# Fourth pair's q and k converted in the transfer, and new copy and slot orders, in an attention kernel that feeds a two-layer product

## The chip, the cores and the metric

The kernel runs on one core of a Trainium2 chip. The metric is device time of one execution in microseconds (us), the median of the runs, lower is better. Times inside an execution come from a profile of one execution, counted from the start of its span.

## What is computed

There are 8 batches of 8 heads, 576 positions and 64 elements to a head. For each head:

```
cum    = cumsum(max(s, 0))
scores = q @ k.T / 8 + min(-(cum[i] - cum[j]), 0)     # only j <= i
x      = softmax(scores) @ v                          # heads side by side: 4608 x 512
h      = x @ w_in                                     # 512 -> 2048
out    = (h * clip(h + 3, 0, 6) / 6) @ w_out          # 2048 -> 512
```

Inputs and output are float32.

## The kernel before, in words

**Pairs and slots.** The work goes by pairs of heads, 32 of them, four to a batch (`PPB` = 4). The loop over `p` (L718) has one slot for each pair. In slot `p` the kernel computes the scores of pair `p` for head 0 and then head 1, its exponentials, the product with the values (`av`, one head behind), the division (`norm`), the transposed x (`transpose_x`), and it prepares q and k of pair `p+1` (`get(0)` for q, `get(1)` for k). Slots count from 0: the fifth slot is `p == 4`, the eighth is `p == 7`.

**The two-layer product.** From slot 4 on, `group()` puts one piece of it between the pieces of attention, by a list written out by hand (`plan`, L505) and, when it is used up, by what is ready. A piece is either `m1` (four matmuls into a bank `ph`, then a Relu on ScalarE into `tr` and a product on VectorE into `gT`) or `m2` (four matmuls into a bank `po`).

**Ways of q and k.** `flat(p)` (L104) says which of two layouts a pair has. A flat pair is loaded as float32 in pieces of 64 elements by SyncE into `raw` (L119) and cast to float16 `tok` by `cast_qk` (L182), on GpSimd unless another engine is given. Pairs below `PPB` are flat and so are those from `NPE` = 11 on. The others are loaded by GpSimd's queue with the conversion in the transfer, straight into `tok`, six positions to a partition on 96 partitions (L114). TensorE transposes a flat pair with five transposes of 128 (L226) for each of q and k, another with six of 96 (L233); pairs from 11 on are transposed by a DMA (`crossbar_qk`, L263). Then q and k are copied from PSUM, or from the DMA's `jt`, into `qk`. A flat pair needs two copies each, by `order` (L203 to L215), for the even and odd blocks. The others need two each at L250, for the even and odd positions, and the first of k is always ScalarE's (L247). `spread` (L267) is the name of the copies from `jt`.

**Bias rows.** Sums of s are computed for 32 heads at a time by `cum1` to `cum6`: a clip, a scan on VectorE (`cum2`), and a split into float16 parts in `rows_of`. The first set is made at the start (L674 to L693), the second in slots 10 to 13 (L763 to L776). `load_aug` (L139) brings a pair's rows into `qk`, by 2 transfers.

**Banks.** The transposes of q and k and of x go to PSUM banks by `t_bank` (L198): while `m2` has not begun, one of two banks `po` if the caller asks for the other one, else the bank `t`, which has one buffer.

**Queues.** The schedule is manual: each engine works its instructions off in the order of the program, and a DMA issue stands in the queue of the engine that issues it. At the start, GpSimd has the casts of the second pair, the values of the first, the third pair's casts, the second pair's values, the issues of the fifth pair (L709 to L714), then in slot 1 the bias rows of the fifth pair and the fourth pair's casts (L729, L730), and in slot 2 the first part of `w_in`. SyncE has bias rows, third pair, values and fourth pair (L700 to L708).

**The start.** ScalarE clips a part of s (L684) and casts the first pair (L688). VectorE makes the sums, and `pick` (L665) the rows in a form for pair 0. The first pair's q and k are each copied half by VectorE and half by ScalarE (L695, L696).

Of the kernel before, what the change touches and what calls it, by code (L numbers as in the profile page):

```python
# [18 lines left out]
def kernel(  # L19
# [10 lines left out]
    nc = tc.nc  # L30

    B, H, SEQ, D = q.shape
# [6 lines left out]
    PPB = H // 2  # L39
# [4 lines left out]
    NPE = 2 * PPB + 3  # L44
    NQK = 4
    NVA = 3
    NPROD = 2 * PPB
# [54 lines left out]
    toks = {}  # L102

    def flat(p):  # L104
        return p < PPB or p >= NPE

    def load_qk(p, i, eng=nc.sync):
        b, h0 = p // PPB, 2 * (p % PPB)
# [68 lines left out]
    def cast_qk(p, copy=nc.gpsimd.tensor_copy):  # L177
        tok = work.tile([128, 24 * D], F16, tag="tok", bufs=4, name="tok")
        toks[p] = tok[:, 0 : 18 * D]
        for i in range(2):  # L180
            c = slice(9 * D * i, 9 * D * (i + 1))
            copy(out=toks[p][:, c], in_=raws[p % NRAW][:, c])  # L182

    def cast_v(p):
        vraw, va = vraws[p % NRAW], vas[p % NVA]
        nc.gpsimd.tensor_copy(out=va[:, :, 0:4, 0:64], in_=vraw[:, :, 0:4, :])  # L186
        nc.gpsimd.tensor_copy(out=va[0:64, :, 4, 0:64], in_=vraw[0:64, :, 4, :])
# [10 lines left out]
    def t_bank(other, name):  # L198
        if not done[2] and other:
            return psum.tile([128, 640], F16, tag="po", bufs=2, name=name)  # L200
        return psum.tile([128, 640], F16, tag="t", name=name)
# [15 lines left out]
    def transpose(p, i, copies=(nc.vector.tensor_copy, nc.vector.tensor_copy)):  # L217
        transpose_out(p, i, transpose_in(p, i), copies)

    def transpose_in(p, i):  # L220
        tok = toks[p]
        pt = t_bank(i == 1, "pt")
        if flat(p):
            for c in range(5):
                c0 = 512 * i + 128 * c
                nc.tensor.transpose(  # L226
                    pt[:, 128 * c : 128 * (c + 1)], tok[:, c0 : c0 + 128], ident
                )
            return pt
        for hh in range(2):  # L230
            for c in range(3):
                n = 96 * (3 * hh + c)
                nc.tensor.transpose(  # L233
                    pt[:, n : n + 96],
                    tok[:, i, hh, 2 * c : 2 * c + 2, :].rearrange("p e d -> p (e d)"),
                    ident[0:96, 0:96],
                )
        return pt

    def transpose_out(  # L240
        p, i, pt, copies=(nc.vector.tensor_copy, nc.vector.tensor_copy)
    ):
        qk = qks[p % NQK]
        if flat(p):
            order(qk, i, pt.rearrange("p (t c) -> p t c", c=128), i, copies)
            return
        copies = (nc.scalar.copy if i else copies[0], copies[1])  # L247
        for par in range(2):
            to = qk[0:64, 0, i, par : par + SEQ]
            copies[par](  # L250
                out=bass.AP(
                    to.tensor,
                    to.offset,
                    [list(to.ap[0]), [2 * SPAD + 64, 2], [6, 96], [2, 3]],
                ),
                in_=pt[64 * par : 64 * par + 64, 0:SEQ].rearrange(
                    "p (h c t) -> p h t c", h=2, c=3
                ),
            )
# [381 lines left out]
    def cum2(n):  # L641
        C["c"] = work.tile([128, SEQ], F32, tag="c8", bufs=1, name="c8")
        nc.vector.tensor_tensor_scan(
            out=C["c"], data0=one.to_broadcast([128, SEQ]), data1=C["p"], initial=0.0, op0=ALU.mult, op1=ALU.add
        )
# [39 lines left out]
        out=C["p"][:, 304:SEQ], in_=C[0][:, 304:SEQ], func=AF.Relu, scale=8.0  # L685
    )
    cum2(0)
    cast_qk(0, nc.scalar.copy)  # L688
    cum3(0, V)
    nc.gpsimd.tensor_copy(out=rows_of[0][0:32, 0, 0:SEQ], in_=C["c"][0:32])  # L690
    cum4(0, V)
    cum5(0, V)
    cum6(0, V)  # L693
    pick(0)
    transpose(0, 0, (V.tensor_copy, nc.scalar.copy))  # L695
    transpose(0, 1, (V.tensor_copy, nc.scalar.copy))  # L696
    warm(NWARM[1])
    for g in range(1, 2 * NROW):
        pick(g)
# [2 lines left out]
        load_qk(2, i)  # L702
    load_aug(2, nc.sync)
    load_v(1, nc.sync)
    for i in range(2):
        load_qk(3, i)
    load_v(2, nc.sync)
    load_aug(3, nc.sync)  # L708
    cast_qk(1)  # L709
    cast_v(0)  # L710
    cast_qk(2)
    cast_v(1)
    for i in range(2):
# [4 lines left out]
    for p in range(NP):  # L718
        nxt = p + 1 < NP
        if NPE <= p + 3 < NP:  # L720
            for i in range(2):
                load_qk(p + 3, i)
        def qk_ahead():
            if PPB < p + 3 < NPE:
                for i in range(2):
                    load_qk(p + 3, i)

        if p == 1:
            load_aug(4, nc.gpsimd)  # L729
            cast_qk(3)  # L730
        elif p == 2:
            load_w_in(0)
            cast_v(2)
            qk_ahead()
        elif p == 3:
            cast_v(3)
            load_w_in(1)
            cast_v(4)
            qk_ahead()
            load_aug(5, nc.gpsimd)  # L740
        elif p:
            qk_ahead()
            if NPE <= p + 2 < NP:
                cast_qk(p + 2)
                crossbar_qk(p + 2)
            for fn, c in {
                4: ((I, 2),),
                5: ((I, 3),),
                6: ((U, 0), (U, 1), (U, 2), (U, 3)),
                7: ((U, 4), (U, 5), (U, 6), (U, 7)),  # L750
            }.get(p, ()):
                fn(c)
            if nxt:
                cast_v(p + 1)
            if NPROD <= p + 2 < NPROD + NQK:
                set_stair((p + 2) % NQK, nc.gpsimd.tensor_copy)
            if p + 2 < NP:
                load_aug(p + 2, nc.gpsimd)
        if p + 3 < NP:
            load_v(p + 3, nc.sync)  # L760
        if p == 2:
            nc.sync.dma_start(out=stair_sb, in_=stair_dram.ap())
        if p == 10:  # L763
            load_s(1, (nc.sync,) * 4)
            fill(nc.gpsimd, rows_of[1][:, 0, :], 1.0)
        if p == 11:
            cum1(1, nc.gpsimd)
        if p == 12:
            cum2(1)
            nc.gpsimd.tensor_copy(out=rows_of[1][0:32, 0, 0:SEQ], in_=C["c"][0:32])  # L770
        if p == 13:
            cum3(1, nc.gpsimd)
            cum4(1, nc.gpsimd)
        if p == 13:
            cum5(1, nc.gpsimd)
            cum6(1, nc.gpsimd)  # L776

        def get(i):
            if p + 1 < NPE:
                transpose(p + 1, i)  # L780
            elif nxt:
                spread(p + 1, i)

        if p < PPB:
            scores(p, 0, 0)
            scores(p, 0, 1)
            get(0)
            scores(p, 0, 2)
            corner(p)
            if p:  # L790
                av(p - 1, 1, 0)
                av(p - 1, 1, 1)
                norm(p - 1, 1)
            get(1)
            scores(p, 1, 0)
            scores(p, 1, 1)
            av(p, 0, 0)
            scores(p, 1, 2)
            if p:
                transpose_x(p - 1)  # L800
            av(p, 0, 1)
            norm(p, 0)
            continue

        if p == PPB:
            early[0] = False
            scores(p, 0, 0)
            av(p - 1, 1, 0)
            av(p - 1, 1, 1)
            norm(p - 1, 1)  # L810
            m1_begin(0, 0, NKC - 1)
            scores(p, 0, 1)
            transpose_x(p - 1)
            m1_begin(0, 1, NKC - 1)
            pt = transpose_in(p + 1, 0)
            scores(p, 0, 2)
            group()
            group()
            transpose_out(p + 1, 0, pt)
        else:  # L820
            if p == NPROD:
                nc.vector.tensor_scalar(
                    out=masks, in0=shut, scalar1=65504.0, scalar2=None, op0=ALU.add
                )
            scores(p, 0, 0)
            get(0)
            group()
            scores(p, 0, 1)
            av(p - 1, 1, 0)
            group()  # L830
            scores(p, 0, 2)
            av(p - 1, 1, 1)
            norm(p - 1, 1)
            group()
        corner(p)
        group()
        if p > NPE:
            x_done[0] = p - 1
        scores(p, 1, 0)
        if p < NPROD - 1:  # L840
            get(1)
            group()
        else:
            if p <= NPROD:
                transpose_x(p - 1)
            group()
            get(1)
        scores(p, 1, 1)
        av(p, 0, 0)
        if PPB < p < NPROD - 1:  # L850
            transpose_x(p - 1)
        elif p > NPROD:
            crossbar_x(p - 1)
        group()
        scores(p, 1, 2)
        group()
        av(p, 0, 1)
        norm(p, 0)
        group()
# [40 lines left out]
```

## Time and profile before

| what | before |
|---|---|
| time, median of 3 runs | 362.35 us (361.83 to 363.53) |
| span of the profiled execution | 361.3 us |
| mean granted TensorE clock | 0.994 |
| DMA moved | 51.60 MB, mean 143 GB/s |
| issue to landing, `raw` q by SyncE | 3.9 us (median) |
| issue to landing, `tok` q by GpSimd | 5.7 us (median) |
| issue to landing, `w_in` part by GpSimd | 9.3 us (median) |

In the profile, engines are PE (TensorE matmul), PEld (its weight load), DVE (VectorE), ACT (ScalarE), POOL (GpSimd) and SP (SyncE); a q behind the name is its sequencer. A line such as `L451 PE MATMUL ph<-xT,w_in_sb` names the code line, the engine, the operation, what it writes and what it reads. Square brackets tell how long the engine was idle ahead of it and what released it. Where a view merges several instructions, x2 is their number.

### The profile page before, as it was taken

The numbers are of one execution on the slowest core, as the hardware profiler recorded it, in microseconds if no ns is written. First come the engines' busy times: TensorE is split into PE (matmuls) and PEld (weight loads), VectorE is DVE, ScalarE is ACT, GpSimd is POOL, SyncE is SP. The second block draws the span as 40 slices with busy tenths as digits, with TensorE's granted clock in tenths as the row PEclk, the third lists the DMA queues.
The fourth block names the chain that finished last, engine by engine and source line by source line (L and its number), as shares of the span: only waits on it lengthen the run. The fifth ranks groups of instructions, "written<-read, shape, count | busy, mean of one in ns | idle before, by whom it ended". The sixth has DMA issues, their size and how long they took to land.

```text
span 361.3 us, 7738 instructions
## 1 busy us (share of the span) xinstructions
PE 348.6 (96%) x2919; PEld 192.9 (53%) x2919; DVE 250.5 (69%) x545; ACT 218.2 (60%) x382; POOL 131.3 (36%) x224
## 2 busy tenths in 40 slices
PE   8879999999999999999999999999999999999995
PEld 3666665555555555555555555555555444444442
DVE  8656997797898878677768777778674644544531
ACT  3757997577666666666666666666665343344310
POOL 5495679973656343515242515252000000000000
PEclk9989999999999999999999999999999999999999
DMA  9899999959999999999897969695122101101111
GB/s 182 170 175 216 217 208 204 182 129 174 179 220 173 226 176 216 193 169 183 181 184 172 199 150 197 158 206 141 21 76 20 58 2 58 59 2 58 58 59 60
DMA packets 152078, 51.60 MB, mean 143 GB/s; under 512 B 139864, under 2 KB 147080, under 8 KB 152040
## 3 DMA queue, kind: packets, MB, share of 16 engines
q1 hardware_dynamic: 141640, 43.74, 60.7%
q0 software_dynamic: 8992, 6.79, 11.7%
q10 hardware_dynamic: 1408, 0.57, 0.7%
q8 instruction: 23, 0.38, 0.5%
q14 instruction: 15, 0.12, 0.1%
HBM read 37.36 MB, written 9.44 MB: 130 GB/s over the span
## 4 chain that ended last, share of the span: by engine, by line
PE 84%; DVE 6%; DMA 4%; SPq 2%; POOL 1%; issue 1%; ACT 1%; POOLq 0%; DVEq 0%; ACTq 0%
PE po L478 33%; PE ph L451 32%; PE O L385 7%; PE S L315 6%; PE S L304 3%; DMA raw<-in_q_dram 2%; DMA jt<-tok 1%; DVE qk L250 1%; DVE gT L467 1%; DVE x L408 1%; DVE qk L210 1%; PE pt L233 1%; DMA vraw<-in_v_dram 1%; PE ptx L422 1%; SPq L119 1%
## 5 line engine op out<-in xcount | busy, mean ns | idle before, releaser
L467 DVE SCALAR_TENSOR_TENSOR gT<-tr,ph 128x512 f16<-128x512 f32 x144 | 98.8, 687 | 77.7 <-ACT tr L466 76.6
L451 PE MATMUL ph<-xT,w_in_sb 128*128 128x512 f16 x576 | 147.9, 379 | 0.5 <-DVE gT L467 0.4
L478 PE MATMUL po<-w_out_sb,gT 128*128 128x512 f16 x576 | 145.8, 379 | 0.0
L466 ACT ACTIVATE tr<-ph,bias 128x512 f32<-128x512 f32 x144 | 98.8, 687 | 73.6 <-PE ph L451 71.4
L334 ACT ACTIVATE P<-S 128x512 f16<-128x512 f32 x192 | 111.7, 595 | 45.9 <-PE S L304 25.0
L451 PEld LDWEIGHTS <-w_in_sb 128*128 128x128 f16 x576 | 51.7, 97 | 44.8 <-issue 0.7
L478 PEld LDWEIGHTS <-gT 128*128 128x128 f16 x576 | 50.0, 98 | 45.8 <-issue 0.2
L182 POOL CAST tok<-raw 128x576 f16<-128x576 f32 x48 | 32.3, 678 | 98.9 <-DMA raw<-in_q_dram 88.6
L315 PE MATMUL S<-qk 68*128 68x448 f16 (+3 forms) x256 | 49.4, 274 | 0.0
L385 PE MATMUL O<-va,P 128*128 128x65 f16 x896 | 48.4, 194 | 0.0
L385 PEld LDWEIGHTS <-P 128*128 128x128 f16 x896 | 39.9, 98 | 13.7 <-DVE qk L210 0.2
L315 PEld LDWEIGHTS <-qk 68*128 68x128 f16 x256 | 23.7, 99 | 22.9
L408 DVE TENSOR_TENSOR x<-O,rl 128x320 f16<-128x320 f32 x64 | 31.5, 491 | 2.2
L210 DVE COPY qk<-jt 64x768 f16<-64x768 f16 x84 | 31.6, 376 | 1.6
L142 POOL DMA_DIRECT2D qk<-rows_of x56 | 32.5, 582 | 0.0
L494 DVE TENSOR_SCALAR ob<-po 128x512 f32<-128x512 f32 (+1 forms) x36 | 24.3, 675 | 8.2 <-PE po L478 7.7
L304 PEld LDWEIGHTS <-qk 128*128 128x128 f16 (+1 forms) x256 | 19.4, 98 | 16.5 <-DVE qk L210 2.8
L304 PE MATMUL S<-qk 128*128 128x128 f16 (+1 forms) x256 | 25.6, 221 | 2.1 <-DVE qk L210 1.6
L186 POOL CAST va<-vraw 128x512 f16<-128x512 f32 x32 | 20.5, 641 | 11.2 <-PE O L385 7.3
L336 DVE TENSOR_TENSOR P<-P,shut 128x512 f16<-128x512 f16 x48 | 22.4, 467 | 2.0 <-ACT P L334 1.5
L250 DVE COPY qk<-pt 64x576 f16<-64x576 f16 x21 | 16.7, 801 | 2.0 <-ACT qk L250 1.6
L407 DVE RECIPROCAL rl<-O 128x5 f32<-128x5 f32 x64 | 12.1, 190 | 6.0 <-PE O L385 5.9
(71 smaller groups left out, 177.8 us busy)
## 6 DMA issues: line engine op xcount, KB each, us to landing
out_dram<-ob SPq DMA_DIRECT2D x35, 256.0 KB, 2.0
vraw<-in_v_dram SPq DMA_DIRECT2D x64, 128.0 KB, 4.9
raw<-in_q_dram SPq DMA_DIRECT2D x25, 288.0 KB, 3.9
raw<-in_k_dram SPq DMA_DIRECT2D x24, 288.0 KB, 4.4
w_in_sb<-in_moe_w_in_dram POOLq DMA_DIRECT2D x4, 512.0 KB, 9.3
w_out_sb<-in_moe_w_out_dram POOLq DMA_DIRECT2D x8, 256.0 KB, 8.5
vraw<-in_v_dram SPq DMA_DIRECT2D x32, 32.0 KB, 3.5
tok<-in_q_dram POOLq DMA_DIRECT2D x7, 144.0 KB, 5.7
```

Of the source, the lines that this page charges most:

```text
L142: eng.dma_start(out=qks[p % NQK][64:68, hh, :, 64 * hh : 64 * hh + SEQ], in_=rows_of[g // 32].rearrange("(r g) i t -> g r i t", g=32)[g % ...
L182: copy(out=toks[p][:, c], in_=raws[p % NRAW][:, c])
L210: copies[par](out=qk[0:64, :, i, 128 * par : 128 * par + 256 * n].rearrange("p h (s two c) -> p h s two c", two=2, c=128)[:, :, :, 0, :], ...
L304: mm(S[:, c], lhsT=kT[rows, c], rhs=qT[rows, c], start=(j == 0 and not by_product), stop=(j == 3),)
L315: mm(S[:, c : c + w], lhsT=kT[0:68, 128 * j : 128 * (j + 1)], rhs=qT[0:68, 128 * (j + 1) : SEQ], start=(c == 0), stop=(c != 0 and p >= NROW),)
L334: nc.scalar.activation(out=pt[:, c], in_=S, func=AF.Exp, scale=0.125)
L385: mm(o[:, i, :], lhsT=lhsT, rhs=va[:, hh, j, 0:65], **kw)
L408: nc.vector.tensor_tensor(out=X[p][:, :, hh, :], in0=o[:, :, 0:64], in1=rl.to_broadcast([128, 5, 64]), op=ALU.mult,)
L451: mm(ph, lhsT=w_in_sb[:, kc, ft * 128 : (ft + 1) * 128], rhs=xT[:, kc, n * 512 : (n + 1) * 512], start=(kc == 0), stop=(kc == NKC - 1),)
L466: nc.scalar.activation(out=tr, in_=ph, func=AF.Relu, bias=bias3[:, 0:1])
L467: nc.vector.scalar_tensor_tensor(out=gTs[n][:, ft, :], in0=tr, scalar=6.0, in1=ph, op0=ALU.min, op1=ALU.mult)
L478: mm(po, lhsT=gTs[n][:, ft, t4 * 128 : (t4 + 1) * 128], rhs=w_out_sb[:, ft, :], start=(ft == 0), stop=(ft == NFT - 1),)
```

## The change

The fourth pair (`p == 3`) leaves the flat layout: it is loaded with the conversion in the transfer, after the first pair's values are cast, and has no casts on GpSimd. In the first pair all of q is copied by ScalarE and all of k by VectorE; a cast of bias rows moves from GpSimd to ScalarE. In slot 4, a copy of the next q goes ahead of the first piece of the two-layer product and the first values' product goes ahead of the second head's scores. Slot 7 gets the order of slots 5 and 6, with the next k transposed ahead of a piece and x transposed after the values' product; the bank of the next k is changed for it. From slot 10 on, the copies of the next k go ahead of a piece. The second set of bias sums is begun a slot sooner. The purpose is to have fewer waits in the first slots and in those where the sums are made.

```diff
@@ -102,7 +102,7 @@
     toks = {}
 
     def flat(p):
-        return p < PPB or p >= NPE
+        return p < PPB - 1 or p >= NPE
 
     def load_qk(p, i, eng=nc.sync):
         b, h0 = p // PPB, 2 * (p % PPB)
@@ -219,7 +219,7 @@
 
     def transpose_in(p, i):
         tok = toks[p]
-        pt = t_bank(i == 1, "pt")
+        pt = t_bank(i == 1 and p != NPROD, "pt")
         if flat(p):
             for c in range(5):
                 c0 = 512 * i + 128 * c
@@ -238,14 +238,14 @@
         return pt
 
     def transpose_out(
-        p, i, pt, copies=(nc.vector.tensor_copy, nc.vector.tensor_copy)
+        p, i, pt, copies=(nc.vector.tensor_copy, nc.vector.tensor_copy), pars=(0, 1)
     ):
         qk = qks[p % NQK]
         if flat(p):
             order(qk, i, pt.rearrange("p (t c) -> p t c", c=128), i, copies)
             return
         copies = (nc.scalar.copy if i else copies[0], copies[1])
-        for par in range(2):
+        for par in pars:
             to = qk[0:64, 0, i, par : par + SEQ]
             copies[par](
                 out=bass.AP(
@@ -685,15 +685,15 @@
         out=C["p"][:, 304:SEQ], in_=C[0][:, 304:SEQ], func=AF.Relu, scale=8.0
     )
     cum2(0)
+    nc.scalar.copy(out=rows_of[0][0:32, 0, 0:SEQ], in_=C["c"][0:32])
     cast_qk(0, nc.scalar.copy)
     cum3(0, V)
-    nc.gpsimd.tensor_copy(out=rows_of[0][0:32, 0, 0:SEQ], in_=C["c"][0:32])
     cum4(0, V)
     cum5(0, V)
     cum6(0, V)
     pick(0)
-    transpose(0, 0, (V.tensor_copy, nc.scalar.copy))
-    transpose(0, 1, (V.tensor_copy, nc.scalar.copy))
+    transpose(0, 0, (nc.scalar.copy,) * 2)
+    transpose(0, 1)
     warm(NWARM[1])
     for g in range(1, 2 * NROW):
         pick(g)
@@ -702,12 +702,12 @@
         load_qk(2, i)
     load_aug(2, nc.sync)
     load_v(1, nc.sync)
-    for i in range(2):
-        load_qk(3, i)
     load_v(2, nc.sync)
     load_aug(3, nc.sync)
     cast_qk(1)
     cast_v(0)
+    for i in range(2):
+        load_qk(3, i)
     cast_qk(2)
     cast_v(1)
     for i in range(2):
@@ -727,7 +727,6 @@
 
         if p == 1:
             load_aug(4, nc.gpsimd)
-            cast_qk(3)
         elif p == 2:
             load_w_in(0)
             cast_v(2)
@@ -760,15 +759,15 @@
             load_v(p + 3, nc.sync)
         if p == 2:
             nc.sync.dma_start(out=stair_sb, in_=stair_dram.ap())
-        if p == 10:
+        if p == 9:
             load_s(1, (nc.sync,) * 4)
             fill(nc.gpsimd, rows_of[1][:, 0, :], 1.0)
+        if p == 10:
+            cum1(1, nc.gpsimd)
         if p == 11:
-            cum1(1, nc.gpsimd)
-        if p == 12:
             cum2(1)
             nc.gpsimd.tensor_copy(out=rows_of[1][0:32, 0, 0:SEQ], in_=C["c"][0:32])
-        if p == 13:
+        if p == 12:
             cum3(1, nc.gpsimd)
             cum4(1, nc.gpsimd)
         if p == 13:
@@ -813,10 +812,11 @@
             transpose_x(p - 1)
             m1_begin(0, 1, NKC - 1)
             pt = transpose_in(p + 1, 0)
+            transpose_out(p + 1, 0, pt, pars=(0,))
+            group()
+            transpose_out(p + 1, 0, pt, pars=(1,))
             scores(p, 0, 2)
             group()
-            group()
-            transpose_out(p + 1, 0, pt)
         else:
             if p == NPROD:
                 nc.vector.tensor_scalar(
@@ -836,18 +836,21 @@
         group()
         if p > NPE:
             x_done[0] = p - 1
+        if p == PPB:
+            get(1)
+            av(p, 0, 0)
         scores(p, 1, 0)
-        if p < NPROD - 1:
+        if p == NPROD:
+            transpose_x(p - 1)
+        if PPB < p < NPROD or p >= NPE - 1:
             get(1)
-            group()
-        else:
-            if p <= NPROD:
-                transpose_x(p - 1)
-            group()
+        group()
+        if NPROD <= p < NPE - 1:
             get(1)
         scores(p, 1, 1)
-        av(p, 0, 0)
-        if PPB < p < NPROD - 1:
+        if p != PPB:
+            av(p, 0, 0)
+        if PPB < p < NPROD:
             transpose_x(p - 1)
         elif p > NPROD:
             crossbar_x(p - 1)
```

## The prediction

> **What bounds the kernel now.** I read five views in this order: the page's sums, TensorE's waits over the whole span, the stretches of two microseconds, the timeline around each wait, and the transfers by tile. The page says where time can come from at all.
>
> ```profile
> PE 348.6 (96%) x2919; PEld 192.9 (53%) x2919; DVE 250.5 (69%) x545; ACT 218.2 (60%) x382; POOL 131.3 (36%) x224
> ...
> PE pt L226 <- POOL tok L182: 2.1, 2, 1.9
> PE S L304 <- DVE qk L210: 1.6, 3, 0.7
> PE ptx L422 <- DVE x L408: 1.4, 3, 0.9
> ...
> PE ph L451 <- DVE gT L467: 0.4, 1, 0.4
> PE S L304 <- ACT qk L210: 0.4, 1, 0.4
> ```
>
> The first line is busy time by engine, the others are TensorE's waits (total, times, longest). TensorE is busy in 348.6 of 361.3 us, so the edits can only remove part of 12.7 us of idle time, some 4.3 of it behind the last matmul and 1.2 ahead of the first, plus any time in which TensorE is busy but slow. The stretches show that there is such time, and only after the largest wait (columns: stretch, length, PE, PEld, DVE, ACT, POOL busy, granted clock, DMA share, GB/s):
>
> ```profile
> 18.00:20.00 2.00, 1.82 (x31) 1.27 (x29) 1.90 (x6) 1.88 (x4) 1.91 (x4) 1.00 0.92 190
> 20.00:22.00 2.00, 0.31 (x4) 0.23 (x4) 0.20 (x1) 0.79 (x2) 2.00 (x4) 1.00 1.13 166
> 22.00:24.00 2.00, 1.79 (x28) 1.67 (x27) 1.17 (x3) 0.77 (x2) 2.00 (x5) 0.67 1.29 170
> 24.00:26.00 2.00, 2.00 (x19) 1.45 (x18) 1.47 (x3) 0.77 (x2) 2.00 (x5) 0.50 1.09 161
> 26.00:28.00 2.00, 2.00 (x35) 1.69 (x34) 1.21 (x4) 1.56 (x4) 0.60 (x1) 0.98 1.24 211
> ```
>
> The reader is to see an idle stretch at 20 to 22, then four microseconds at a clock of 0.67 and 0.50. The slow clock costs 2 x 0.33 + 2 x 0.50 = 1.7 us on top of the 2.1 of waiting. The timeline shows what TensorE waited for:
>
> ```profile
> 18.33 0.81 POOL L114 DMA_DIRECT2D tok<-in_q_dram  x1
> ...
> 19.13 0.68 POOL L114 DMA_DIRECT2D tok<-in_k_dram  x1
> ...
> 19.78 1.18 POOL L142 DMA_DIRECT2D qk<-rows_of  x2
> ...
> 20.96 1.28 POOL L182 CAST tok<-raw 128x576 f16<-128x576 f32 x2
> ...
> 21.69 0.40 PE L226 MATMUL pt<-ident,tok 128*128 128x128 f16 x4 [1.87 <-POOL tok L182]
> ```
>
> The casts of the fourth pair stand last in GpSimd's queue, behind four DMA issues. Two further waits concern the change: slot 7 (58.60, transposing x, 0.88 us), where the product of L408 stood behind two qk copies and a gT, and slot 12 (103.68, 0.65 us), where two qk copies stood behind a gT and a mask.
>
> ```profile
> 58.60 0.45 PE L422 MATMUL ptx<-ident,x 128*128 128x128 f16 x5 [0.88 <-DVE x L408]
> ...
> 103.68 0.66 PE L304 MATMUL S<-qk 128*128 128x128 f16 x4 [0.65 <-DVE qk L210]
> ```
>
> From 112 us on TensorE is nearly without waits, so what is gained before it should reach the end almost whole.
>
> **What the Trainium skill says.** *TensorE: Matmul & The Clock Gate*, Part 1 (The HAM clock gate), says that the clock is halved after an idle window of about 3.4 us and given back after a busy one. The trace agrees on the half clock, but the idle time that brought it here was only about 2 us. *DMA: Bandwidth & Descriptors*, SWDGE vs HWDGE vs iDMA, says that a transfer that converts has to be issued by GpSimd; the trace shows the later pairs so, at 0.66 us an issue. *ScalarE: Activation LUTs*, What ACT_TABLE_LOAD costs, prices an operation with immediate operands at 186 ns + 0.833 ns an element: 0.67 for 576, and the trace has 0.671 for the casts at L182. *GPSIMD Engine Reference*, Specifications, says that GpSimd shares SBUF interfaces with VectorE; the trace fits: picking a row set took 0.66 us during a GpSimd cast and 0.35 after it.
>
> **The change, part by part.**
>
> *Fourth pair converted in the transfer.* Removed: two SyncE issues (0.53 + 0.56 us), two GpSimd casts (1.28 together). Added: two GpSimd issues after the first value casts. Those casts ended at 11.62, and GpSimd then waited 2.03 us for the third pair's q, until 13.64. Two issues by 0.66 to 0.81 end at 12.9 to 13.2, inside that gap, so they hold up nobody on GpSimd. Transfers of this kind landed 3.7 to 7.5 us after issue; the k issue, at about 12.4, gives 16.1 to 19.9. TensorE asks for q at 19.6 and for k over a microsecond later. I take landed in time. The pair now has the layout of L233 and L250: three VectorE copies of 0.81 for four of about 0.50, 0.4 us more, and 0.81 more on ScalarE. The price of a slot of that form is visible: slot 3 has it, 26.65 to 30.78, 4.13 us from mask matmul to mask matmul. Slot 2 took 18.93 to 26.65, 7.72. So slot 2 gains 7.72 - 4.13 = 3.6 us. This agrees with 2.1 + 1.7 less some 0.2 of added copies.
>
> *First pair.* ScalarE's rows copy is 32x576, 0.67 us from 6.0, and moves ScalarE's casts from 6.38 to about 6.7, their end from 7.80 to 8.1. The fifth q transpose needs k's cast, so q is in PSUM at 8.35; ScalarE copies it in 0.83 (768 elements, the page's price) + 0.60 (the trace's L210), to 9.8. VectorE may lose the contention at L659 (0.80 us, against 0.46 for the wider L648), picks until 9.2 to 9.6, then copies k in 0.57 + 0.50, until 10.3 to 10.7. Before, the two engines took turns at q and at k, and ScalarE stood 2.26 us for VectorE; the scores went on at 11.31. That is 0.6 to 1.0 us sooner. But then slot 1 asks for the third pair at 14.8 to 15.2 instead of 15.77, and its k cast, gated by a transfer issued behind a row load, ended at 16.1. I give this part nothing, and 0.4 at best. The GpSimd issues can delay that transfer by a few tenths.
>
> *Order in slot 4 (the fifth).* A copy of 0.81 goes ahead of the first gT, into 1.94 us in which VectorE waited for ScalarE (before 35.75). The values' product fills TensorE while get(1) is copied. Waits there: 0.20 on P and 0.44 on gT. I take 0.5.
>
> *Order in slot 7 (the eighth).* Transposing x goes behind scores and values as in slots 5 and 6, which show no such wait. The k transposes take the bank t instead of po; that bank has a single buffer, but its q copies end at 57.2, before the need. Of 0.88 I take 0.8.
>
> *Second bias sums sooner, spreads sooner.* The scan (1.37 us of VectorE) moves from slot 12 to 11, where VectorE had waits of 0.79 and 0.46, and GpSimd's cast and subtraction from 13 to 12. From slot 10 on the two copies of L210 stand ahead of a gT, not behind it. The waits are 0.65 + 0.26 at 103.68 and 111.92. I take 0.7. A gT that is some 1.0 us later costs nothing, since TensorE turns to a second ph bank.
>
> *What the earlier slots run into.* The transfers are busy from 20 to 70 us without a gap (share 1.2 to 1.3 in each stretch). The bias rows of pair 5 are the tightest: issued at 33.20, landed 5.4 later, at 38.6, used at 39.33, so 0.7 of slack. They stand on GpSimd behind the casts of pair 4's values, which waited for vraw until 30.02 and 31.45. That chain moves by 1.3 us (the casts gone) to 3 (two SyncE issues and 2304 small packets gone as well); I take 2.2. TensorE asks 3.6 + 0.5 = 4.1 sooner. New wait: 4.1 - 0.7 - 2.2 = 1.2 us, with ends of 0.4 and 2.1. The first weights (issued 22.17, landed 6.6 later, used 31.82) have 3.0 of slack, so they come about in time.
>
> Sum: 3.6 + 0 + 0.5 + 0.8 + 0.7 - 1.2 = 4.4 us. 362.35 - 4.4 = 358.0.
>
> **Rivals.**
>
> *All waits vanish.* The loads move with the rest, slot 4 gives 0.64, slot 7 0.88, slots 12 and 13 0.9, and the start 0.3: 3.6 + 0.64 + 0.88 + 0.9 + 0.3 = 6.3, 356.0 us. For it speaks that 2304 packets of 256 bytes go; against it, the unbroken load on the queues.
>
> *The transfer takes the cast's place.* The fourth pair lands after 20 us, or pairs 5 and 6 wait for rows and weights, so that half of slot 2's gain goes: 1.8 + 0.5 + 0.5 + 0.3 - 1.2 = 1.9, 360.5 us. For it: GpSimd's transfers took over 7 us at 24 us. Against it: they took 3.7 to 4.4 at 18.33.
>
> *Slower.* The converting transfer delays the third pair's k and first values, and an idle window at 14 to 16 halves the clock there (1.7 lost). The fourth pair lands so late that slot 2's wait stays whole, with 0.4 of added copies, and spreads ahead of gT cost TensorE 0.05 in each of 21 slots (1.0). Slots 4 and 7 give 0.8: 362.35 + 1.7 + 0.4 + 1.0 - 0.8 = 364.7 us. For it: the gap from 10 to 12 us (TensorE busy 0.93 of 2) would be followed by loads closer together. Against it: that gap did not slow the clock.
>
> **How the numbers follow.** Forecast 0.65, all vanish 0.15, transfer takes the cast's place 0.15, slower 0.05. The range is 356.0 to 360.8: it reaches the second and nearly all of the third, and takes in the ends of the new wait (0.4 and 2.1). Same means 360.5 to 364.2. Faster gets the first two and about half of the third, 0.87; same gets the other half, 0.08; slower the last, 0.05.
>
> **What would show it.** Right: no wait on a cast for the fourth pair, clock 1.00 from 20 to 28 us, slot 2 near 4.1 us, a short new wait of the first scores of slot 5 for its rows, no wait of 0.88 at slot 7's x. Wrong: a wait of TensorE for tok behind a transfer in slots 1 or 2, a clock below 1.00 after it, or waits for qk copies past 112 us.

## The result, and the profile after

| | before | changed |
|---|---|---|
| median of 4 runs | 362.49 us (361.83 to 363.53) | 361.68 us (361.53 to 361.94) |
| ratio, 95% interval | | 0.9976 (0.9951 to 1.0000) |
| span of the profiled execution | 361.3 us | 360.1 us |
| end of the last matmul | 356.9 us | 356.5 us |

The forecast was 358.0 us, 4.4 faster. It came out 0.8 faster, with an interval that ends at no change. Two later measurements of the same changed kernel, e9 and e13 among the experiments, gave 0.9923 (0.9895 to 0.9951) and 0.9915 (0.9881 to 0.9948), 2.8 and 2.5 us by their medians. So the sign was right, and the size was between a fifth and two thirds of the forecast. All three belong to the result. In the first, with four runs of each kernel, the kernel before is some 0.8 us faster than in the other two (363.36 and 363.24) and the changed kernel 1.0 slower (360.61 and 360.79); how much of this is chance and how much the chip is open. Medians below leave out one run of e1 and one of e2 that lay far above the others (452.95 and 934.39 us).

The place that the forecast turned on went as it said. The stretches that answer to those of before, same columns (stretch, length, PE, PEld, DVE, ACT, POOL busy, granted clock, DMA share, GB/s):

```profile
18.00:20.00 2.00, 1.21 (x24) 1.05 (x24) 0.61 (x2) 0.72 (x2) 1.88 (x4) 1.00 0.37 87
20.00:22.00 2.00, 2.00 (x41) 1.75 (x40) 1.91 (x5) 1.66 (x5) 2.00 (x4) 1.00 0.93 126
22.00:24.00 2.00, 1.74 (x30) 1.29 (x28) 1.90 (x4) 2.00 (x6) 2.00 (x5) 1.00 1.21 204
24.00:26.00 2.00, 2.00 (x40) 1.72 (x40) 1.92 (x6) 1.63 (x4) 2.00 (x5) 1.00 1.23 195
```

The idle stretch at 20 and the slow clock behind it are gone, but at 18 to 20 TensorE is busy for only 1.21 us of 2, a new idle time. TensorE's waits over the whole span name it, and others that are new (in all, times, longest):

```profile
PE O L385 <- POOL va L186: 1.8, 2, 1.5
PE ph L451 <- DMA w_in_sb<-in_moe_w_in_dram: 1.6, 1, 1.6
...
PE S L304 <- DVE qk L210: 1.1, 2, 0.9
PE S L304 <- DMA qk<-rows_of: 1.0, 1, 1.0
PE O L385 <- DVE x L408: 0.7, 1, 0.7
PE pt L233 <- DVE xT L427: 0.7, 1, 0.7
PE ptx L422 <- DVE x L408: 0.5, 2, 0.3
```

The fourth pair's cast is out of the list. In its place stand the second pair's values (1.5), the first weights (1.6), bias rows (1.0), an x transpose's copy (0.7) and a division (0.7). The first part of the profile's page puts it together: TensorE was busy 348.6 us before and 347.0 after, since the slow clock is gone, and yet the last matmul ended only 0.4 sooner, so its waits grew by 1.2.

A ledger by slot shows where. Slots are cut at the first score matmul of a pair (L304); the idle time of TensorE is the length less its busy time. Before, slots 1, 2, 3, 4, 5 with 6, 7 with 8, and 9 to 14:

```profile
15.33:19.15 3.82, 3.82 (x68) 3.15 (x66) 3.26 (x9) 3.26 (x8) 2.33 (x5) 1.00 0.90 196
19.15:26.87 7.72, 5.64 (x68) 4.32 (x67) 3.88 (x11) 3.82 (x8) 7.46 (x13) 0.78 1.15 172
26.87:31.12 4.25, 3.90 (x69) 3.00 (x68) 3.96 (x9) 3.91 (x9) 0.61 (x1) 1.00 1.27 214
31.12:39.33 8.21, 7.55 (x85) 4.76 (x85) 5.61 (x12) 6.06 (x13) 7.33 (x13) 1.00 1.28 224
39.33:53.86 14.53, 14.48 (x169) 9.47 (x169) 13.60 (x25) 12.86 (x25) 10.09 (x17) 1.00 1.25 208
53.86:72.33 18.47, 17.40 (x182) 10.54 (x181) 13.40 (x27) 12.04 (x22) 18.04 (x26) 1.00 1.06 193
72.33:121.09 48.76, 47.77 (x453) 27.52 (x452) 42.86 (x93) 34.89 (x64) 28.26 (x45) 1.00 1.00 178
```

The changed kernel, the same slots:

```profile
14.40:19.97 5.57, 3.98 (x68) 3.22 (x67) 3.54 (x9) 3.65 (x8) 2.51 (x5) 1.00 0.84 166
19.97:24.15 4.18, 3.92 (x69) 3.07 (x68) 3.96 (x9) 3.84 (x9) 4.18 (x8) 1.00 1.08 169
24.15:28.39 4.24, 3.91 (x70) 3.02 (x69) 4.06 (x9) 3.87 (x9) 2.24 (x5) 1.00 1.23 195
28.39:39.10 10.71, 7.72 (x85) 4.84 (x85) 7.13 (x13) 6.42 (x13) 6.85 (x12) 1.00 1.26 211
39.10:53.41 14.31, 14.31 (x168) 9.40 (x169) 12.59 (x24) 12.43 (x24) 11.02 (x17) 1.00 1.14 185
53.41:71.29 17.88, 17.21 (x182) 10.58 (x181) 13.24 (x27) 11.92 (x22) 16.64 (x25) 1.00 1.09 190
71.29:120.68 49.39, 47.78 (x453) 27.48 (x452) 43.91 (x93) 35.12 (x64) 29.72 (x46) 1.00 1.02 186
```

Read the second column. Slot 1 starts 0.9 sooner and is 1.75 longer. Slot 2 falls from 7.72 to 4.18, to the hundredths near the 4.13 that the forecast took from slot 3. Slot 4 starts 2.7 sooner and is 2.5 longer, so slot 5 starts only 0.2 sooner. Slots 7 and 8 give 0.6, slots 9 to 14 lose 0.6.

The three new waits for transfers in the timeline of the changed kernel (start, length, what; in brackets the wait):

```profile
18.79 0.41 PE L385 MATMUL O<-va,P 128*128 128x65 f16 x8 [1.51 <-POOL va L186]
...
30.86 0.82 PE L451 MATMUL ph<-xT,w_in_sb 128*128 128x512 f16 x3 [1.61 <-DMA w_in_sb<-in_moe_w_in_dram]
...
39.10 0.38 PE L304 MATMUL S<-qk 68*128 68x128 f16 x4 [1.00 <-DMA qk<-rows_of]
```

Their times from issue to landing, first weights and then the sixth pair's rows, before:

```profile
DMA to landing us min/median/max: 6.6/6.6/6.6
...
DMA to landing us min/median/max: 5.3/5.4/5.6
```

and in the changed kernel:

```profile
DMA to landing us min/median/max: 9.5/9.5/9.5
...
DMA to landing us min/median/max: 7.6/7.8/8.0
```

The weights were issued 0.8 us sooner (21.33 for 22.17) and the rows 2.2 sooner (30.96 for 33.20), as the forecast had it for the rows, and both landed no sooner: the weights at 30.8 for 28.8, the first of the rows' two transfers at 39.0 for 38.8.

### The profile page after: what moved, and what is told of

Same layout as the page of the kernel before. It is cut to its first block, busy times and chain, and to the rows that moved or that the text cites. A ratio compares the mean times of both kernels' runs of the same rounds, so it can differ in the third digit from the quotient of the medians.

```text
span 360.1 us, 7743 instructions
## 1 busy us (share of the span) xinstructions
PE 347.0 (96%) x2921; PEld 191.9 (53%) x2921; DVE 252.1 (70%) x544; ACT 219.3 (61%) x384; POOL 130.9 (36%) x223
## 4 chain that ended last, share of the span: by engine, by line
PE 84%; DMA 5%; DVE 5%; POOL 2%; SPq 1%; issue 1%; ACT 1%; POOLq 0%
PE po L478 33%; PE ph L451 32%; PE O L385 7%; PE S L315 6%; PE S L304 4%; DMA qk<-rows_of 2%; DMA raw<-in_q_dram 2%; DMA vraw<-in_v_dram 1%; DVE gT L467 1%; DVE P L336 1%; DVE x L408 1%; PE pt L233 1%; DVE qk L210 1%; POOL tok L114 1%; PE ptx L422 1%
## 5 line engine op out<-in xcount | busy, mean ns | idle before, releaser
L466 ACT ACTIVATE tr<-ph,bias 128x512 f32<-128x512 f32 x144 | 99.0, 688 | 72.9 <-PE ph L451 70.7
L182 POOL CAST tok<-raw 128x576 f16<-128x576 f32 x46 | 31.0, 675 | 97.9 <-DMA raw<-in_q_dram 86.1
L304 PEld LDWEIGHTS <-qk 128*128 128x128 f16 (+1 forms) x256 | 19.2, 98 | 16.5 <-DVE qk L210 2.1
L304 PE MATMUL S<-qk 128*128 128x128 f16 (+1 forms) x256 | 25.1, 219 | 2.2 <-DVE qk L210 1.1
L336 DVE TENSOR_TENSOR P<-P,shut 128x512 f16<-128x512 f16 x48 | 24.6, 512 | 2.4 <-ACT P L334 2.2
L250 DVE COPY qk<-pt 64x576 f16<-64x576 f16 x24 | 19.3, 803 | 2.9 <-ACT qk L250 2.0
```

The source lines that it names most:

```text
L304: mm(S[:, c], lhsT=kT[rows, c], rhs=qT[rows, c], start=(j == 0 and not by_product), stop=(j == 3),)
L466: nc.scalar.activation(out=tr, in_=ph, func=AF.Relu, bias=bias3[:, 0:1])
```

## The experiments

**Theory.** The fourth pair's wait was removed, but in the first 70 us TensorE runs against transfers that land when they land. What it gains in slot 2 it waits for in slots 1, 4 and 5. **Rival.** The gain is real, and the new orders of the other parts cost it. Behind each "Measured" stand the ratio to the kernel before on the same chip, its 95% interval, and the median.

**The fourth pair alone (e1).** On the kernel before:

```diff
-        return p < PPB or p >= NPE
+        return p < PPB - 1 or p >= NPE
...
+    for i in range(2):
+        load_qk(3, i)          # behind cast_v(0); not on SyncE, no cast_qk(3)
```

> The kernel before with one part of the change: the fourth pair converted in the transfer. Theory 'saturated transfers' (the wait and the slow clock at 20 to 26 us go, but the first weights and the fifth and sixth pairs' rows land no sooner than before, so TensorE waits for them in slots 4 and 5): 361.0 to 362.3 us, clock 1.00 at 22 to 26 us, a wait of 1 to 2 us for w_in or rows at 28 to 40 us. Rival 'the other parts took it back' (the part is worth its 3.6 us and the new orders cost 2 to 3): 358.5 to 359.5 us.

Measured: 0.9974 (0.9948 to 1.0001), 362.38 us beside 363.67 for the kernel before on that chip. Clock 1.00, and waits of 1.2 for values, 0.6 for w_in and 1.5 for rows. This is the theory's outcome, 0.1 above its range: of the 3.6 us of slot 2, some 1.3 are left at the end, with none of the other parts present.

**All but the fourth pair (e2).** On the changed kernel, the reverse of that diff.

> The changed kernel with the fourth pair as before (float32 load by SyncE, casts in slot 1). Saturated transfers: the part was worth little, so 361.5 to 362.6 us, with the wait for the cast and the slow clock back, and no wait for w_in. Rival 'the other parts took it back': 364 to 365.5 us.

Measured: 0.9970 (0.9952 to 0.9989), 362.19 us. The wait for the cast (2.1 in all) and the slow clock are back, w_in is not waited for. The other parts do not cost 2 to 3 us; they give 1.5. The rival falls. The 1.3 of e1 and the 1.5 of e2 together are about what the later measurements found for the whole (2.8 and 2.5).

**Fewer transfers, in both kernels (e3, e4).**

```diff
-        if p + 3 < NP:
+        if NPE <= p + 3 < NP:
             load_v(p + 3, nc.sync)
```

Pairs 3 to 10 use the values of pairs 0 to 2, which leaves out 2304 KB of transfers and nothing of the work of the engines.

> The changed kernel without the transfers of the values of pairs 3 to 10 (2304 KB less in the first 65 us; these pairs use the values of pairs 0 to 2 that lie in the buffers, so the output is another). Saturated transfers: w_in's first part and the rows of the sixth pair land 1.5 to 3 us sooner, the waits of 1.6 and 1.0 us go, 358 to 359.5 us. Rival 'the other parts took it back': 361.3 to 361.9 us.

> The kernel before with the same transfers left out (pairs 3 to 10 use the values of pairs 0 to 2). Saturated transfers: TensorE did not wait for transfers here, so only little changes, 361.5 to 362.5 us, and the distance to the changed kernel without them is 3 us or more. Rival: the same 361.5 to 362.5, with a distance below 1 us.

Measured: 0.9896 (0.9856 to 0.9936) and 0.9960 (0.9941 to 0.9979), 359.53 and 362.70 us, each just above its range. The waits for w_in and rows are gone in e3. The distance of the two is 3.2 us.

**Loads in the order of need (e5).** On the changed kernel:

```diff
-            load_w_in(0)
+            for c in range(2):      # the same 512 columns in two halves
+                nc.gpsimd.dma_start(out=w_in_sb[:, :, 256 * c : 256 * (c + 1)], ...)
...
             cast_v(3)
+            load_aug(5, nc.gpsimd)
             load_w_in(1)
-            cast_v(4)
             qk_ahead()
-            load_aug(5, nc.gpsimd)
+            cast_v(4)
```

> The changed kernel with the same transfers in another order on GpSimd: the first part of w_in comes in two halves of 256 columns, and in slot 3 the sixth pair's rows and the seventh pair's q and k are issued ahead of the cast of the fifth pair's values. Theory 'saturated transfers, needed late': the waits of 1.6 us for w_in and 1.0 for rows in slots 4 and 5 shrink below 0.5 together, 1.5 to 2.5 us faster than the changed kernel, 359.3 to 360.3 us where it has 361.7. Rival 'whole volume sets the pace': the waits move to later loads, less than 0.6 us faster.

Measured: 0.9925 (0.9881 to 0.9970), 360.76 us; no wait for w_in or rows above 0.15 us. The waits went as 'needed late' had it, the time did not: it is above 359.3 to 360.3, and no better than the changed kernel's 360.61 and 360.79 on other chips. TensorE idled 2.35 us in slot 1 here, and slot 2 ran at a clock of 0.67.

**The second pair's values sooner as well (e6).**

```diff
-    load_aug(2, nc.sync)
     load_v(1, nc.sync)
+    load_aug(2, nc.sync)
```

> The kernel of the run before this one, and in addition SyncE issues the second pair's values ahead of the third pair's rows. Needed late: the wait of 1.5 us for those values in slot 1 falls to 0.5 or less, and another 0.5 to 1.0 us is gained. Whole volume sets the pace: slot 2 starts sooner, but slots 4 and 5 start at the same time as without this.

Measured: 0.9929 (0.9908 to 0.9950), 360.26 us. The wait for values is 1.1, more than was expected; slot 5 starts at 36.4 in the profile (e5: 38.0, in part by its slow clock in slot 2). The 0.5 us of time lie inside the intervals.

**Late orders undone (e7).** On the changed kernel, `load_s`, `cum1` to `cum4` a slot later again, and

```diff
-        if PPB < p < NPROD or p >= NPE - 1:
+        if PPB < p < NPROD:
             get(1)
         group()
-        if NPROD <= p < NPE - 1:
+        if p >= NPROD:
             get(1)
```

> The changed kernel with its two late parts undone: from slot 10 the copies of the next k stand behind a piece again, and the second bias sums are made a slot later, as in the kernel before. If these parts gave the 0.7 us that were forecast, this run is 0.5 to 0.9 us slower than the changed kernel; if they only moved the wait on VectorE (0.87 us at slot 12 in the place of 0.65 and 0.26), it is within 0.3 us.

Measured: 0.9947 (0.9929 to 0.9965), 361.31 us. The changed kernel was not on this chip, so by time this is open: on the other chips it stood at 0.9976, 0.9923 and 0.9915. By one pair of profiles the late parts are worth about 0.9 us: TensorE is idle 1.75 us in slots 12 to 14 here and 0.88 in e9. The wait is another than in the kernel before, for a DMA that transposes x:

```profile
109.84 0.38 PE L451 MATMUL ph<-xT,w_in_sb 128*128 128x512 f16 x1 [1.68 <-DMA xT<-x]
```

**The fourth pair's transfer later (e8).** On the changed kernel:

```diff
-    for i in range(2):
-        load_qk(3, i)
     cast_qk(2)
+    for i in range(2):
+        load_qk(3, i)
```

> The changed kernel with the two converting issues of the fourth pair behind the casts of the third pair instead of ahead of them, some 3 us later. If this transfer pushed back the second pair's values (landed 17.6 to 18.0, after 16.2 in the kernel before), the values land 1 us or more sooner and their wait of 1.5 us in slot 1 falls below 0.7; the fourth pair then lands at 19 to 21 us and may make TensorE wait for it. By time within 0.6 us of the changed kernel, since slots 4 and 5 wait for other transfers. If it did not push them back, the wait stays at 1.2 to 1.7 us.

Measured: 0.9910 (0.9870 to 0.9950), 360.75 us. The first two issues of the second pair's values landed at 15.6 and 16.2 us instead of 17.6 and 18.0, with the issues at the same time to 0.1 us. From issue to landing, in the changed kernel and then in e8:

```profile
DMA to landing us min/median/max: 5.1/5.1/5.2
...
DMA to landing us min/median/max: 3.1/3.2/3.2
```

The cast of them and the product that waits for it, in e8:

```profile
17.06 0.64 POOL L186 CAST va<-vraw 128x512 f16<-128x512 f32 x1
...
17.75 0.41 PE L385 MATMUL O<-va,P 128*128 128x65 f16 x8
```

There is no bracket behind the product now, where it had 1.51. That the converting transfer pushed the values back is shown. Slot 2 starts a microsecond sooner (18.93 for 19.97), TensorE does not wait for the fourth pair, and ahead of slot 5 the rows are waited for again (1.4), with w_in 0.5. By time nothing is left of it beside 360.61 and 360.79.

**The changed kernel beside the reordered loads (e9, e10).** e10 is e6 with e8's edit.

> The changed kernel itself, on the chip of the three runs beside it. Both theories: 0.996 to 0.999 of the kernel before. It is the measure for the other runs: 1 to 2 us above the kernel with the loads in the order of need (e10) by 'needed late', within 0.6 by 'whole volume sets the pace'.

> The changed kernel with all reorderings of loads at once: w_in's first part in halves, rows of the sixth pair ahead of the cast in slot 3, second values ahead of the third pair's rows, fourth pair's issues behind the third pair's casts. Needed late: 0.989 to 0.993 of the kernel before, and waits for values, w_in and rows below 1.0 us together. Whole volume sets the pace: 0.995 or more.

Measured: 0.9923 (0.9895 to 0.9951), 360.61 us, and 0.9923 (0.9893 to 0.9953), 360.29 us. The times can't tell them apart, and e9 came out faster than either theory had it. The profile shows why so little is left. In e10, slot 5 begins at 35.7 (e9: 38.3) and slot 8 at 59.0 (61.3); slot 9 begins at 69.2 (70.6). TensorE's waits of e10:

```profile
PE O L385 <- POOL va L186: 0.9, 1, 0.9
PE pt L233 <- DVE xT L427: 0.9, 1, 0.9
PE po L478 <- DMA w_out_sb<-in_moe_w_out_dram: 0.8, 1, 0.8
```

Of the 2.6 us that slot 5 gained, slot 8 took 1.0 back, 0.8 of it waiting for the second weights. The wait moved to the next load.

**The same load order without the change (e11).** e5's edit on the kernel before.

> The kernel before with only the two reorderings of slots 2 and 3 (w_in's first part in halves; rows of the sixth pair and the seventh pair ahead of a cast). Here TensorE did not wait for these, so by 'needed late' it is within 0.3% of the kernel before; if the order of loads is worth something by itself, 0.994 or less.

Measured: 0.9992 (0.9966 to 1.0018), 363.38 us. By time the order of loads is worth nothing by itself.

**Slot 7 as before (e12).** On the changed kernel:

```diff
-        pt = t_bank(i == 1 and p != NPROD, "pt")
+        pt = t_bank(i == 1, "pt")
...
-        if p == NPROD:
+        if NPROD - 1 <= p <= NPROD:
             transpose_x(p - 1)
-        if PPB < p < NPROD or p >= NPE - 1:
+        if PPB < p < NPROD - 1 or p >= NPE - 1:
             get(1)
         group()
-        if NPROD <= p < NPE - 1:
+        if NPROD - 1 <= p < NPE - 1:
             get(1)
...
-        if PPB < p < NPROD:
+        if PPB < p < NPROD - 1:
             transpose_x(p - 1)
```

> The changed kernel with slot 7 in the order and with the bank of the kernel before. If the new order gave 0.8 us, this run is 0.5 to 1.0 us slower than the changed kernel (e9). If it moved the wait from slot 7's x (0.88 us) to slot 8's k transposes (0.67 us, behind the copy of x on VectorE), it is within 0.4 us; in the trace a wait near 0.9 at slot 7 is back and the one at slot 8 is below 0.3.

Measured: 0.9943 (0.9923 to 0.9963), 361.15 us, on the chip of e9. The medians are 0.5 apart, inside the intervals. The traces say which wait goes against which, first e12:

```profile
56.62 0.45 PE L422 MATMUL ptx<-ident,x 128*128 128x128 f16 x5 [0.88 <-DVE x L408]
```

then e9:

```profile
67.67 0.42 PE L233 MATMUL pt<-ident,tok 96*128 96x96 f16 x6 [0.76 <-DVE xT L427]
```

Slots 7 and 8 together last 18.5 us in e12 and 18.0 in e9: 0.5 us gained of the 0.88, with the wait of slot 8 in place of the rest.

**Volume and order, all on one chip (e13 to e16).** The changed kernel; it with few values (e3's edit); e10 with few values; the kernel before with few values.

> The changed kernel a third time, beside the three runs below on the same chip: 0.992 to 0.998 of the kernel before by either theory, the measure for them.

> The changed kernel without the values' transfers of pairs 3 to 10 (they use the values of pairs 0 to 2). 'Volume sets the pace': 2 to 3 us below the changed kernel (e13), last w_out landed near 62 us, not near 68. 'Order sets the pace': below it by less than 1.

> The kernel with the loads in the order of need (e10) without the same transfers (pairs 3 to 10 use the values of pairs 0 to 2). 'Volume': within 0.7 us of e14, since with less volume the order no longer matters, and no wait for w_out in slot 8. 'Order': 1 us or more below e14.

> The kernel before without the same transfers (pairs 3 to 10 use the values of pairs 0 to 2). 'Volume': less than 1.5 us below the kernel before and at least 2 us above e14, so that the change is worth more where the transfers leave room. If both kernels gain the same from it, the change's worth does not depend on the volume.

Measured: 0.9915 (0.9881 to 0.9948), 0.9901 (0.9861 to 0.9940), 0.9857 (0.9824 to 0.9891) and 0.9975 (0.9957 to 0.9994); medians 360.79, 359.95, 358.58 and 362.54 us. Slot 4 of e14 shows what the volume does there:

```profile
28.56:36.51 7.95, 7.56 (x85) 4.78 (x85) 6.55 (x12) 5.93 (x13) 6.91 (x12) 1.00 1.24 196
```

It is 7.95 us long with 0.39 idle, and so in e3, e10 and e15 as well; in the changed kernel it lasted 10.71, 9.42 (e9) and 9.37 (e13), and in e12 and e7, which are the same up to slot 6, 9.05 and 8.28. The last second weights landed at 66.9 to 70.7 us in all runs with the whole volume, the kernel before and the reordered ones alike, and at 60.4 to 62.4 in the five with few values. So the volume sets when that load lands, and slot 4 can be freed by less volume or by another order.

That the volume sets a landing shows best in e9 and e14, which issued the sixth pair's rows at the same moment, first e9, then e14:

```profile
28.28 1.19 POOL L142 DMA_DIRECT2D qk<-rows_of  x2
...
DMA to landing us min/median/max: 9.4/9.6/9.9
```

```profile
28.19 1.18 POOL L142 DMA_DIRECT2D qk<-rows_of  x2
...
DMA to landing us min/median/max: 5.5/5.7/5.9
```

The first transfer landed at 38.1 and at 34.1 (at 34.9 in e3, with few values too, issued at 28.3). In the five traces with the changed kernel's early slots (its own, e7, e9, e12, e13) it was issued from 28.3 to 31.0 and landed from 37.0 to 39.0; in the kernel before it was issued at 33.2 and landed at 38.8. So issues up to 5 us sooner brought landings at most 1.8 sooner. In e10, where it goes ahead of other loads, it was issued at 24.9 and landed at 30.9.

By time the verdict is weaker. e14 is only 0.8 us below e13, short of the 2 to 3 expected, with runs from 358.45 to 361.43. e15 is 2.2 below e13 and 1.4 below e14. Both came out as 'order' had it, though e15 gains with volume and order together what neither gave alone. e16 is where 'volume' had it, 0.7 below the kernel before and 2.6 above e14. The change is worth 2.6 us with few values (362.54 - 359.95) and 2.4 with all on this chip (363.24 - 360.79): that it is worth more where the transfers leave room is not shown by these times. Change and load order together, with few values, are worth 4.0 (362.54 - 358.58), near the 4.4 that were forecast, though the order alone gave nothing (e11).

## Why the prediction was wrong

**Slot 2: right for the profiled execution.** 7.72 became 4.18 us, 3.5 where 3.6 was forecast. The transfer landed in time in every run of it, and TensorE never waited for the fourth pair.

**"What is gained before it should reach the end almost whole": the step that failed.** It was corrected for one new wait of 1.2 us only. The runs show that waits for transfers in slots 1 and 4 took most of it back: in the profile of the result slot 5 starts 0.2 us sooner. Two terms that the sum put at nothing were waits of 1.6 us each, and the third was right by luck.

*Slot 1, forecast 0.* TensorE was idle there for 1.6 us (2.1 in e9, 1.75 in e13), for the second pair's values. The forecast looked at the third pair's k, and said "a few tenths". The values, which stand behind it, were not costed at all. e8 shows a cause: with the converting transfer 4 us later, they land 2 us sooner. The Trainium skill says in *DMA: Bandwidth & Descriptors*, Issuing engines are not separate DMA queues, that transfers from all issuing engines share the same 16 DMA engines; the trace of e8 agrees, with those 2 us for a transfer that GpSimd issued on one that SyncE issued, and the forecast should have used it here. The sooner start of 0.9 us (within the 0.6 to 1.0 forecast) went into this wait as well: e2, which has it without the transfer, is idle for 0.95 in slot 1 (0.8 of it for the values), and e1, which has the transfer without it, for 1.20.

*The first weights, forecast "about in time".* This took a landing of 6.6 us from the trace of before, and it was 9.5: 1.6 us of waiting. The same operation took 9.1 to 10.3 us at three other places of that trace. The smallest of four was used. It was not out of reach (6.1 in e7, 6.5 in e9, 8.0 in e12 and 8.5 in e13), but it could not be counted on.

*The rows, forecast 1.2 us (0.4 to 2.1).* It was 1.0 in the profile of the result, right in place, and in size by luck. The forecast let TensorE ask 4.1 us sooner and the rows land 2.2 sooner. They landed no sooner, and TensorE, held up in slots 1 and 4, asked only 1.2 sooner (38.1 for 39.33): two errors that cancel. The slack was also read a little large, 0.7 us for 0.5, since the first transfer took 5.6 us and landed at 38.8.

Together slot 4 was idle 2.99 us instead of 0.66, so it took 2.3 more where the sum had 1.2 - 0.5 = 0.7. In e9 and e13 it was 1.0 more. In e9, 1.3 of it ended when the rows landed: the view puts this wait to a division on VectorE, but the sixth pair's last copy had ended at 36.0, the first rows landed at 38.1, and TensorE went on at 38.27. The landings change from run to run by as much as the gain at stake. This may be why three measurements of one kernel gave 0.8 to 2.8 us; it is not shown.

**The slow clock: right in the profile, doubtful in the time.** The granted clock of the kernel before was not 0.994 in each run. Beside e1 to e4 there are 47 runs of it with clocks from 0.987 to 1.000. The 18 below 0.9935 have a median of 363.9 us, the 10 above 0.997 one of 363.9; the correlation is 0.04. A half per cent of clock would be 1.8 us, and nothing like it is seen. Yet inside one execution the loss is there. The kernel before with few values has a trace of each kind, slot 2 of e4 and then of e16 (same columns):

```profile
19.60:25.57 5.97, 4.22 (x67) 3.15 (x66) 3.89 (x11) 3.83 (x8) 4.31 (x8) 1.00 1.16 186
```

```profile
19.10:26.62 7.52, 5.65 (x67) 4.32 (x66) 3.88 (x11) 3.82 (x8) 6.96 (x13) 0.77 1.16 201
```

TensorE is idle for 1.75 and 1.87 us, and only in e16 does the slow clock follow. Slot 2 is 1.55 longer there, and slot 5 begins 1.1 later (39.09 for 38.02), though slot 2 had begun 0.5 sooner. So the 1.7 us are path time in an execution that has them, but not every execution has them. In e11, the kernel before with other loads, slot 2 idles 2.10 at a clock of 1.00 and takes 6.33: there 2.2 us could be gained, not 3.6. The forecast took one profile for all runs. Why the times of 47 runs show no effect is open.

**Slot 4's order, forecast 0.5:** 0.27, from the 0.66 idle before to 0.39 in e3, e10 and e14, where no load is waited for.

**Slot 7's order, forecast 0.8:** 0.5, by one pair of profiles and by medians inside their intervals. The wait at x went, and part of it came back in slot 8, where k's transposes and x's share the bank t and the copy of x on VectorE stands behind a mask.

**Late orders, forecast 0.7:** against the kernel before, next to nothing (idle in slots 12 to 14: 0.99 before, 0.87 after). Against the changed kernel without them, about 0.9 by the profile. In e7 another wait stands there (1.68 us); that the sooner slots bring it is not shown. The wait for qk copies came back as 0.87 us in slot 12, where the two copies took 1.77 us beside GpSimd's casts (0.65 at 99.20, with no cast beside them).

**The rivals.** "The transfer takes the cast's place", at 0.15 and 360.5 us, was nearest. Its mechanism was half right: rows and weights were waited for, the fourth pair was not, and it lacked the second pair's values. The range ended at 360.8, which holds two of the three medians of the changed kernel, by 0.01 and 0.2 us, but not the first.

## What to carry to other kernels

Before you count a removed wait as gained, list every load that the next slots use, with its landing and its first use, and take the longest time to landing that the trace has for its kind, not the one beside it. A transfer moved to an idle spot of one queue runs against the loads that are issued behind it on other queues. Where a stretch is full of transfers, as from 20 to 68 us here, an edit that speeds up the engines may only move the wait to the next load: look for what can be sent in the order of need, and for what need not be sent. And before you count a slow clock as lost time, look whether other executions of the kernel have it.

## What the runs showed of the hardware that was not expected

- The granted clock of the kernel before varied from 0.987 to 1.000 between runs, with no effect on its time that 47 runs would show. In other kernels a lower clock went with a longer time: the 11 runs of e12 above 0.997 have a median of 360.59 us, its 9 at 0.995 or below one of 361.91. Which of the two is the cause is open: in these traces the slow clock also follows an idle time.
- An idle time of some 2 us on TensorE was followed by a slow clock in some executions and not in others. Slot 2 had a mean clock of 0.78 with 2.08 us idle (before), 0.77 with 1.92 (e2) and with 1.87 (e16), and 1.00 with 2.10 (e11) and with 1.75 (e4).
- A transfer of a full stretch did not land sooner for being issued sooner: the sixth pair's rows, issued at 28.3 (e9) and 31.0 (the result), landed at 38.1 and 39.0, and with 2304 KB less to transfer, issued at 28.2 (e14), at 34.1.
- A VectorE operation with two tensors in SBUF (L336, 128x512) takes 0.42 us as the median of its 48 executions, and took 1.42 in one beside a GpSimd copy within SBUF. In the changed kernel that one begins inside the copies at 71.51; in the kernel before, the same mask came at the end of them and took 0.44:

```profile
71.51 2.45 POOL L594 COPY qk<-stair_sb 64x1280 f16<-64x1280 f16 x2
...
72.81 1.42 DVE L336 TENSOR_TENSOR P<-P,shut 128x512 f16<-128x512 f16 x1
```

  and in the kernel before:

```profile
71.57 2.45 POOL L594 COPY qk<-stair_sb 64x1280 f16<-64x1280 f16 x2
...
73.85 0.44 DVE L336 TENSOR_TENSOR P<-P,shut 128x512 f16<-128x512 f16 x1
```

  A slot that begins 1 us sooner was enough to move the mask into the copies. The order counted in the two pickings of the forecast, too: the one of 0.35 us was not free of a cast, which began 0.12 behind it (10.67 for 10.55), and the one of 0.66 began 0.4 inside a cast (8.92 for 8.52).
